# Weight loads in longer runs per partition, in a decode block that streams 185.6 MB

## The chip, the cores and the metric

The kernel runs on one core of one Trainium2 chip. The metric is device time in microseconds (us); lower is better. Every time below is a median over executions, and all of them were in the fast state. A kernel and the kernel before were run alternately on the same chip, and a ratio is the mean time of one kernel's fast runs over that of the other's in the same rounds, so it isn't quite the ratio of the medians that are quoted beside it.

## The reference, cut to what matters

One token passes through a conditioned layer norm, grouped-query attention over a long cache, and a gated feed-forward block. All tensors are bf16.

```python
mod = (silu(c) @ w_mod)                    # w_mod 1024 x 6144
h = layernorm(x) * (1 + ca) + sa
q = h @ wq                                 # wq 1024 x 4096: 32 heads of 128
p = softmax(q @ k.T * 128**-0.5)           # k, v: 4 kv heads x 65536 x 128
x = x + ga * ((p @ v) @ wo)                # wo 4096 x 1024
h = layernorm(x) * (1 + cb) + sb
x = x + gb * ((gelu(h @ w_gate) * (h @ w_up)) @ w_down)   # 1024 x 3584, 3584 x 1024
```

The K and V caches are 134.2 MB together; w_mod, wq, wo, gate, up and w_down are the other 51.4 MB. Each byte is read once.

## The kernel before

All large loads are issued by SP, in one order, into ten slots of 16 KB per partition. A load waits until the earlier users of its slots are done. Three small loads (c and x, 2 KB each) are issued by ACT on its own queue.

```python
def plan_load(src, view_fn, slot, site=None, nslot=1):   # nslot neighbouring slots
    ...
    for t in range(slot, slot + nslot):
        if last_job[t] is not None and last_job[t] not in job.prev:
            job.prev.append(last_job[t])
        last_job[t] = job

def issue_ready():                                       # strictly in the planned order
    while issued[0] < len(loads):
        j = loads[issued[0]]
        if any(q.freed is None for q in j.prev):
            return
        SP.wait(*(q.freed for q in j.prev))
        sp.dma_start(j.view, j.src).then_inc(j.tok[0], 16)
        issued[0] += 1
...
act.dma_start(c_in[:, :], c[0].rearrange("(p k) -> p k", p=P)).then_inc(c_sem, 16)      # 16 bytes per partition
act.dma_start(x_in[:, :], A_x[0, 0].rearrange("(p k) -> p k", p=P)).then_inc(x_sem, 16)
act.dma_start(x_row[:, :], A_x[0, 0].rearrange("(j p) -> j p", p=P)).then_inc(in_sem, 16)
wmod_v = w_mod.rearrange("(p k) n -> p k n", p=P)        # rows of one partition are neighbours in HBM
...                                                      # wq, wo, gate and up likewise
```

Since the rows of a partition lie together in HBM, a load of `k:k + n` is one contiguous run of n rows per partition. Before, w_mod takes 1 row (12 KB), wq 2 rows (16 KB), wo 8 (16 KB), gate and up 2 (14 KB). K is loaded in runs of 32 KB into two slots (0-1 and 2-3 in turn), V in runs of 16 KB into slots 4 to 7. TensorE's first instruction waits for x_row (until 10.49 us in the trace), and w_mod follows in the program (12.86 us).

## Time and profile before

| | before |
|---|---|
| time, median of 3 runs | 440.36 us |
| span of the profiled run | 438.8 us |
| load queue, share of 16 DMA engines | 98.8% |
| first weight packet starts / last one ends (packet records) | 1.85 / 435.67 us |

The page of the kernel before: its span, the busy time of each engine, the bytes moved in 40 equal slices, all DMA packets, and the load queue (packets, MB, and the share of the time of 16 engines that its packets took).

```profile
span 438.8 us, 15336 instructions
PE 351.7 (80%) x7107; PEld 318.4 (73%) x7107; DVE 176.2 (40%) x300; ACT 146.4 (33%) x553; POOL 11.7 (3%) x25
GB/s 332 427 435 428 430 429 432 432 433 425 430 445 420 453 414 455 408 445 438 410 448 415 445 419 442 427 435 432 430 437 424 439 423 433 432 427 431 424 425 237
DMA packets 11957, 185.89 MB, mean 424 GB/s; under 512 B 1568, under 2 KB 1568, under 8 KB 1952
q1 hardware_dynamic: 11632, 185.61, 98.8%
```

Apart from the first and the last slice, the rate is about the same in the slices of w_mod and wq (12 and 16 KB runs, the first five) as in those of K and V (single slices stray from 408 to 455, since a packet's bytes are counted whole in the slice where it starts). While loads are queued, differences between these run lengths are too small to be seen here. The table by stretches of this trace has 429 to 436 GB/s in stretches of 40 to 60 us from 20 to 400 us, and the page 424 GB/s over the whole span.

The timeline of TensorE in the kernel before, three parts of it (start, length, engine, line, operation, tiles, count, and in brackets the idle time just before it and what ended that):

```profile
10.49 0.16 PE L463 MATMUL b<-ident,x_row 8*128 8x8 bf16 x1 [10.49 <-DMA x_row<-in_A_x_dram]
12.86 4.78 PE L392 MATMUL kt_ps<-slots,s_pad 128*32 128x512 bf16 x36
...
63.04 1.88 PE L561 MATMUL kt_ps<-ident,slots 128*128 128x128 bf16 x16 [5.08 <-DMA slots<-in_A_k_cache_dram]
...
423.86 1.85 PE L372 MATMUL b<-u_col,slots 128*128 128x1 bf16 x64 [0.49 <-DVE u_col L841]
428.64 1.86 PE L372 MATMUL b<-u_col,slots 128*128 128x1 bf16 x64 [2.93 <-DMA slots<-in_B_w_down_dram]
433.51 2.91 PE L372 MATMUL b<-u_col,slots 128*128 128x1 bf16 x96 [3.01 <-DMA slots<-in_B_w_down_dram]
```

TensorE starts w_mod at 12.86 us, then waits for data. The first transpose of K (L561) waits 5 us for K to land, and the last third of w_down waits 3 us: at these two points data come last, so a lag of TensorE that is shorter than the wait is absorbed there.

The small loads of the kernel before, from the list of DMA issues (last number: us from issue to landing):

```profile
c_in<-in_c_dram ACTq DMA_DIRECT2D x1, 2.0 KB, 4.3
x_in<-in_A_x_dram ACTq DMA_DIRECT2D x1, 2.0 KB, 8.2
```

They are 2 KB each, and take as long as some 1.8 and 3.5 MB of the stream (an estimate, at the page's mean of 424 GB/s).

### The profile page before, as it was taken

How to read it: one execution, taken by the hardware profiler on the slowest of the kernel's cores; microseconds unless marked ns; L12 is line 12 of the kernel's file. 1: busy time of each engine (PE TensorE's matmuls, PEld its weight loads, DVE VectorE, ACT ScalarE, POOL GpSimd, SP SyncE). 2: the span in 40 equal slices, each digit the busy share in tenths (PEclk: the TensorE clock that was granted, in tenths of full speed). 3: DMA queues.
4: the chain of work that ended last, by engine and by line, in shares of the span. 5: the costliest groups of instructions: out<-in, count | busy, mean ns of one | idle time of the engine just before them, and what ended most of it. 6: DMA issues, size and time to landing. Idle time of an engine off the chain costs nothing.

```text
span 438.8 us, 15336 instructions
## 1 busy us (share of the span) xinstructions
PE 351.7 (80%) x7107; PEld 318.4 (73%) x7107; DVE 176.2 (40%) x300; ACT 146.4 (33%) x553; POOL 11.7 (3%) x25
## 2 busy tenths in 40 slices
PE   0547449998989889898799989999989999557554
PEld 0214139998989879798799989899988999434234
DVE  4102013545444644455444466345563365142100
ACT  1000001343435634344613553444654434600000
POOL 8100000000000000000000000000000000000000
PEclk9955555959777986869955899556995597659855
DMA  8999999999999999999999999999999999999995
GB/s 332 427 435 428 430 429 432 432 433 425 430 445 420 453 414 455 408 445 438 410 448 415 445 419 442 427 435 432 430 437 424 439 423 433 432 427 431 424 425 237
DMA packets 11957, 185.89 MB, mean 424 GB/s; under 512 B 1568, under 2 KB 1568, under 8 KB 1952
## 3 DMA queue, kind: packets, MB, share of 16 engines
q1 hardware_dynamic: 11632, 185.61, 98.8%
q8 instruction: 13, 0.21, 0.2%
q10 hardware_dynamic: 304, 0.01, 0.0%
q14 instruction: 8, 0.07, 0.0%
HBM read 185.60 MB, written 0.00 MB: 423 GB/s over the span
## 4 chain that ended last, share of the span: by engine, by line
DMA 60%; PE 35%; DVE 2%; issue 1%; SPq 1%; ACT 1%; POOL 0%
DMA slots<-in_A_v_cache_dram 39%; PE kt_ps L561 18%; DMA slots<-in_A_k_cache_dram 10%; DMA slots<-in_B_w_down_dram 7%; PE b L625 7%; PE sc_ps L581 6%; DMA slots<-in_w_mod_dram 4%; PE kt_ps L392 2%; PE b L605 1%; SPq L234 1%; PE b L372 1%; ACT p_sb L691 1%; PE b L595 1%; DVE kt_sb L751 0%; PE sc_ps L453 0%
## 5 line engine op out<-in xcount | busy, mean ns | idle before, releaser
L561 PE MATMUL kt_ps<-ident,slots 128*128 128x128 bf16 x2048 | 179.5, 258 | 11.0 <-DMA slots<-in_A_k_cache_dram 10.3
L561 PEld LDWEIGHTS kt_ps<-ident,slots 128*128 128x128 bf16 x2048 | 154.9, 118 | 12.7 <-issue 9.8
L660 DVE COPY kt_sb<-kt_ps 128x2048 bf16<-128x2048 bf16 x96 | 117.6, 1225 | 108.6 <-PE kt_ps L561 108.5
L660 ACT ACTIVATE kt_sb<-kt_ps 128x2048 bf16<-128x2048 bf16 x32 | 60.1, 1877 | 183.3 <-PE kt_ps L561 183.3
L625 PE MATMUL b<-p_sb,slots 128*128 128x8 bf16 x2176 | 75.8, 168 | 20.6 <-DMA slots<-in_A_v_cache_dram 11.2
L625 PEld LDWEIGHTS b<-p_sb,slots 128*128 128x128 bf16 x2176 | 69.8, 100 | 23.3 <-DMA slots<-in_A_v_cache_dram 12.3
L691 ACT ACTIVATE p_sb<-sc_ps,mneg 128x64 bf16<-128x64 f32 x256 | 83.5, 560 | 3.9 <-DVE mneg L686 3.9
L691 ACT ACTIVATION_READ_ACCUMULATOR p_sb<-sc_ps,mneg 128x1 f32 x256 | 77.1, 365 | 0.0
L581 PE MATMUL sc_ps<-q_buf,kt_sb 128*128 128x8 bf16 x2112 | 69.9, 167 | 0.5 <-issue 0.5
L581 PEld LDWEIGHTS sc_ps<-q_buf,kt_sb 128*128 128x128 bf16 x2112 | 67.9, 100 | 0.6 <-issue 0.6
L392 PE MATMUL kt_ps<-slots,h_pad 128*32 128x512 bf16 x176 | 17.1, 510 | 14.3 <-DMA slots<-in_A_wq_dram 6.3
L684 DVE TENSOR_REDUCE mg<-b 8x1 f32<-8x128 f32 x32 | 8.9, 279 | 37.1 <-PE b L595 37.1
L679 DVE TENSOR_REDUCE m_col<-sc_ps 128x8 f32<-128x512 f32 x32 | 21.8, 681 | 4.7 <-PE sc_ps L581 4.7
L392 PEld LDWEIGHTS kt_ps<-slots,h_pad 128*32 128x32 bf16 x176 | 5.0, 112 | 24.1 <-DMA slots<-in_A_wq_dram 8.3
L392 PE MATMUL kt_ps<-slots,s_pad 128*32 128x512 bf16 x96 | 12.5, 553 | 9.3 <-DMA slots<-in_w_mod_dram 9.3
L392 PEld LDWEIGHTS kt_ps<-slots,s_pad 128*32 128x32 bf16 x96 | 3.6, 119 | 17.3 <-DMA slots<-in_w_mod_dram 12.6
L605 PE MATMUL b<-negi,mg 8*128 8x8 f32 x66 | 15.8, 309 | 0.0
L605 PEld LDWEIGHTS b<-negi,mg 8*128 8x128 f32 x66 | 12.7, 239 | 2.2
L453 PEld LDWEIGHTS sc_ps<-identf,kt_sb 128*128 128x128 f32 (+1 forms) x48 | 7.6, 204 | 8.2 <-DVE kt_sb L774 4.3
L453 PE MATMUL sc_ps<-identf,kt_sb 128*128 128x128 f32 (+1 forms) x48 | 9.1, 352 | 4.5 <-DVE kt_sb L774 2.4
L686 DVE COPY mneg<-b 128x8 f32<-128x8 f32 x32 | 5.3, 167 | 18.1 <-PE b L605 18.1
L372 PE MATMUL b<-u_col,slots 128*128 128x1 bf16 x224 | 6.6, 165 | 6.5 <-DMA slots<-in_B_w_down_dram 5.9
(97 smaller groups left out, 84.9 us busy)
## 6 DMA issues: line engine op xcount, KB each, us to landing
slots<-in_A_k_cache_dram SPq DMA_DIRECT2D x16, 4096.0 KB, 20.3
slots<-in_A_v_cache_dram SPq DMA_DIRECT2D x32, 2048.0 KB, 26.5
slots<-in_w_mod_dram SPq DMA_DIRECT2D x8, 1536.0 KB, 17.5
slots<-in_A_wq_dram SPq DMA_DIRECT2D x4, 2048.0 KB, 35.2
slots<-in_A_wo_dram SPq DMA_DIRECT2D x4, 2048.0 KB, 32.5
slots<-in_B_w_gate_dram SPq DMA_DIRECT2D x4, 1792.0 KB, 21.9
slots<-in_B_w_up_dram SPq DMA_DIRECT2D x4, 1792.0 KB, 23.6
slots<-in_B_w_down_dram SPq DMA_DIRECT2D x3, 2048.0 KB, 29.1
```

What stands on the lines that cost most here:

```text
L372: ins = pe.matmul(bank[:, j:j + 1], view[:, kk, j * P:(j + 1) * P], rhs[:, k0 + kk:k0 + kk + 1], start=first, stop=True, skip_group_check= ...
L392: ins = pe.matmul(out, pad[:, k, :], jb.view[:, kk, c0:c0 + ROW], start=k <= last_k[0], stop=k >= last_k[1], skip_group_check=True,)
L453: ins = pe.transpose(dst[:, i * w:i * w + n], src[:, a], identf[0:src.shape[0], 0:n])
L561: ins = pe.transpose(kt_ps[:, half * 2048 + t * P:half * 2048 + (t + 1) * P], j_k[i - i % KU].view[:, i % KU * CH + b * TB + t, :], ident[ ...
L581: ins = pe.matmul(sc_ps[:, base + n * REP:base + (n + 1) * REP], kt_sb[:, j % 2, n, :], q_buf[:, j % SITES, :], start=True, stop=True,)
L605: ins = pe.matmul(b6[:, 256:256 + REP], mg8[:, j % 2:j % 2 + 1].to_broadcast([REP, P]), negi[:, :], start=True, stop=True,)
L625: ins = pe.matmul(b7[:, s * REP:(s + 1) * REP], j_v[j].view[:, n, :], p_sb[:, s, n, :], start=(n == 0), stop=(n == CH - 1),)
L660: ev[i % SITES][b].done(act.activation(dst, src, ACT.Copy) if E_ is AC else dve.tensor_copy(dst, src))
L679: m1[s].done(dve.tensor_reduce(m_col[:, j % 2, :].unsqueeze(2), scv, AX.X, ALU.max))
L684: m2[s].done(dve.tensor_reduce(mg8[:, j % 2:j % 2 + 1], b6[0:REP, 32:32 + P], AX.X, ALU.max))
L686: v_mc[j] = DVE.done(dve.tensor_copy(mneg[:, j, :], b6[:, 256:256 + REP]))
L691: ins = act.activation(p_sb[:, s, :, h], scv[:, h, :], ACT.Exp, bias=mneg[:, j, h:h + 1], scale=scale, accum_out=z_all[:, j, h:h + 1],)
```

## The change

Its intent is to give each packet more bytes, so that a fixed cost per packet (about 5 ns by the packet records and runs below) is paid less often: one load takes two or four rows of each partition and fills two slots. K, V and w_down keep their runs.

```diff
-        head = [8, 9, 0, 1, 2, 4, 3, 5, 6, 7, 8, 9]
-        j_mod = [(plan_load(wmod_v[:, k:k + 1, :], flat(1, M6), head[k]), k, 1) for k in range(KD)]
-        j_q = [(plan_load(wq_v[:, k:k + 2, :], flat(2, HQ * DH), head[KD + k // 2]), k, 2) for k in range(0, KD, 2)]
+        head = iter([8, 0, 2, 4, 6, 8])
+        j_mod = [(plan_load(wmod_v[:, k:k + 2, :], flat(2, M6), next(head), nslot=2), k, 2) for k in range(0, KD, 2)]
+        j_q = [(plan_load(wq_v[:, k:k + 4, :], flat(4, HQ * DH), next(head), nslot=2), k, 4) for k in range(0, KD, 4)]
 ...
-            return (plan_load(wo_v[:, k:k + 8, :], flat(8, D), next(tail)), k, 8)
+            return (plan_load(wo_v[:, k:k + 16, :], flat(16, D), next(tail), nslot=2), k, 16)
 ...
-        j_g = [(plan_load(wg_v[:, k:k + 2, :], flat(2, F), next(tail)), k, 2) for k in range(0, KD, 2)]
-        j_u = [(plan_load(wu_v[:, k:k + 2, :], flat(2, F), next(tail)), k, 2) for k in range(0, KD, 2)]
+        j_g = [(plan_load(wg_v[:, k:k + 4, :], flat(4, F), next(tail), nslot=2), k, 4) for k in range(0, KD, 4)]
+        j_u = [(plan_load(wu_v[:, k:k + 4, :], flat(4, F), next(tail), nslot=2), k, 4) for k in range(0, KD, 4)]
 ... (slot numbers of the tail and of w_down to suit)
```

More of the change, by code (lines that the diff above doesn't have):

```diff
@@ L111, in bass_adaLN_cond__gqa_block_cached__geglu_ffn__decode_kernel @@
     NQ = P // QD
-    assert FD % UE == 0 and M6 <= SLOT and KD % 2 == 0
+    assert FD % UE == 0 and M6 <= SLOT and KD % 4 == 0
     assert D == 2 * ROW and HQ * DH == 2 * NQ * ROW and F % ROW == 0 and F <= 2 * NQ * ROW and UE * P == ROW
@@ L263, in kv_src @@
             return h[g][:, cc * CH:(cc + n) * CH, :]
-        head = [8, 9, 0, 1, 2, 4, 3, 5, 6, 7, 8, 9]
-        j_mod = [(plan_load(wmod_v[:, k:k + 1, :], flat(1, M6), head[k]), k, 1) for k in range(KD)]
-        j_q = [(plan_load(wq_v[:, k:k + 2, :], flat(2, HQ * DH), head[KD + k // 2]), k, 2) for k in range(0, KD, 2)]
-        tail = iter([8, 9] + 2 * [0, 1, 2, 3, 4, 5, 6, 7, 8, 9])
+        head = iter([8, 0, 2, 4, 6, 8])
+        j_mod = [(plan_load(wmod_v[:, k:k + 2, :], flat(2, M6), next(head), nslot=2), k, 2) for k in range(0, KD, 2)]
+        j_q = [(plan_load(wq_v[:, k:k + 4, :], flat(4, HQ * DH), next(head), nslot=2), k, 4) for k in range(0, KD, 4)]
+        tail = iter([8, 0, 2, 4, 6, 8])
+        tail_d = iter([0, 1, 2, 3, 4, 5])
         def plan_o(k):
-            return (plan_load(wo_v[:, k:k + 8, :], flat(8, D), next(tail)), k, 8)
+            return (plan_load(wo_v[:, k:k + 16, :], flat(16, D), next(tail), nslot=2), k, 16)
         blank = {}
@@ L288, in emit_all @@
             if i == SITES:
-                j_o = [plan_o(k) for k in range(0, 16, 8)]
+                j_o = [plan_o(k) for k in range(0, 16, 16)]
             if i < NC and i % KU == 0:
@@ L294, in emit_all @@
                 j_v[j] = plan_load(kv_src(vh, j), flat(CH, DH), SITES + j % SITES, vfill[j % SITES])
-        j_o += [plan_o(k) for k in range(16, HQ, 8)]
-        j_g = [(plan_load(wg_v[:, k:k + 2, :], flat(2, F), next(tail)), k, 2) for k in range(0, KD, 2)]
-        j_u = [(plan_load(wu_v[:, k:k + 2, :], flat(2, F), next(tail)), k, 2) for k in range(0, KD, 2)]
+        j_o += [plan_o(k) for k in range(16, HQ, 16)]
+        j_g = [(plan_load(wg_v[:, k:k + 4, :], flat(4, F), next(tail), nslot=2), k, 4) for k in range(0, KD, 4)]
+        j_u = [(plan_load(wu_v[:, k:k + 4, :], flat(4, F), next(tail), nslot=2), k, 4) for k in range(0, KD, 4)]
         j_d = []
@@ L304, in emit_all @@
                 lambda t: t[:, 0:2 * UE * D].rearrange("p (b e n) -> p b e n", b=2, e=UE),
-                next(tail),
+                next(tail_d),
             )
@@ L310, in emit_all @@
             for e, ne in ((0, 2), (2, 1), (3, 1)):
-                jb = plan_load(wd_v[:, b, e:e + ne, :], flat(ne, D), next(tail))
+                jb = plan_load(wd_v[:, b, e:e + ne, :], flat(ne, D), next(tail_d))
                 j_d.append((jb, jb.view, b * UE + e, ne))
```

## The prediction

> **What bounds the kernel now.** DMA traffic. The page's queue table gives the load queue 98.8% of the time of 16 engines over 438.8 us (433.5 us); the table by stretches shows 420 to 438 GB/s in nearly every stretch from 5 to 430 us. [...] The first packet starts at 1.85 us, the last weight packet ends at 435.7 us, so about 5 us lie outside the stream. TensorE (80% busy) is close behind, but the chain of waits is mostly DMA (60%), and the queue stayed full behind its PE parts.
>
> **What longer runs save.** In the trace's packet records one packet is one run of one partition. Median times lie on a line: 8 KB 309 ns, 12 KB 460, 14 KB 535, 16 KB 611, 32 KB 1,213: 36.8 ns per 1,000 bytes plus about 9 ns per packet. So 12 KB already runs at 26.7 bytes/ns against 27.0 at 32 KB. [...] The K cache already uses 32 KB runs; K and V, 73% of the bytes, don't change. The change removes 512 (w_mod) + 256 (wq) + 256 (wo) + 512 (gate, up) = 1,536 packets, 96 per engine, 0.9 us at 9 ns (estimate from the fit), and 12 issues with their semaphore packets (12 per engine, 9 ns each: 0.1 us). Together about 1.0 us. SP's saved issue time (12 x about 0.4 us) is off the path.
>
> **What it costs.**
> - Head: the first w_mod load lands about 3.6 us later, but TensorE started w_mod only at 12.85 us, waiting for other inputs. The last w_mod and wq jobs process twice the rows after landing: +1.9 us at most for wq (16 matmuls took 1.90 us). q is ready near 60.3 us instead of 58.4; the first K transpose waited for K until 63.0. Absorbed.
> - Slots in pairs: issue times against bytes landed show about 2.8 to 4.4 MB still queued at each K and V refill, over 6 us of work. At the tail, the first up load moves from 380.4 to about 385.8 us with some 6 MB queued; the second waits for wo as before (396.2). w_down issues move by up to 4 us with 9 MB queued. No stall.
> - Tail: up's last job has 28 matmuls instead of 14, so w_down's column work starts about 1.7 us later; it had waited for data until 433.5. Absorbed.
>
> **On the critical path:** only the packet overhead, 1.0 us of 440.36.
>
> **Predicted: 439.4 us, 8 in 10 between 438.6 and 440.6.** Chances: faster by over 2% 0.01, within 2% 0.97, slower 0.02.
>
> **What would show it right:** packets down by about 1,700; load-queue busy time from 433.5 to about 432.5 us; 24 KB packets near 913 ns, 28 KB near 1,063; last w_down landing about 1 us earlier; first K transpose still waiting for K near 62 us.
>
> **What would make it wrong:** a stretch with DMA idle near 385 to 415 us, where two-slot loads wait for TensorE; runs cut into shorter packets (no gain); a lower granted clock, so that TensorE lags by more than the queued 6 us; engines that finish more unevenly (their last packets spread over 431.3 to 435.7 us now), so that the slowest gains less than the mean.

## The result, and the profile after

The changed kernel took 439.97 us (six runs, 439.87 to 440.27) against 440.44 us (six runs, 440.32 to 440.66): 0.47 us less, ratio 0.999, 95% interval 0.9978 to 1.0003. The interval of the ratio reaches from 0.97 us less to 0.1 us more: it excludes neither no gain nor, quite, the 1.0 us forecast. That the gain is half of the forecast can't be read from these two medians alone; the packet records suggest why it should be, and runs with a larger effect test it.

The same lines of the page after the change:

```profile
span 438.6 us, 15324 instructions
PE 345.6 (79%) x7107; PEld 315.0 (72%) x7107; DVE 171.9 (39%) x300; ACT 146.4 (33%) x553; POOL 11.7 (3%) x25
GB/s 343 411 442 429 428 432 426 430 432 427 429 435 429 448 420 456 410 445 439 410 451 409 452 409 451 418 433 442 424 434 427 433 430 433 438 434 425 423 424 238
DMA packets 10228, 185.88 MB, mean 424 GB/s; under 512 B 1376, under 2 KB 1376, under 8 KB 1760
q1 hardware_dynamic: 9904, 185.60, 98.8%
```

The load queue has 1,728 packets fewer, exactly 1,536 runs and 12 times 16 semaphore packets (a semaphore packet is a record of 4 bytes that follows a load's data, 16 to a load; in this trace the 16 semaphore updates of c's load come about 0.5 us after its 16 such records, at 10.26 to 10.73 us). The share of busy time didn't move in its last digit, and the last weight packet ends at 435.41 us instead of 435.67.

The timeline of TensorE after the change, at the same places:

```profile
20.18 0.16 PE L464 MATMUL b<-ident,x_row 8*128 8x8 bf16 x1 [20.18 <-DMA x_row<-in_A_x_dram]
20.78 7.09 PE L393 MATMUL kt_ps<-slots,s_pad 128*32 128x512 bf16 x72
...
63.24 1.89 PE L562 MATMUL kt_ps<-ident,slots 128*128 128x128 bf16 x16 [3.37 <-DMA slots<-in_A_k_cache_dram]
...
425.22 1.87 PE L373 MATMUL b<-u_col,slots 128*128 128x1 bf16 x64 [0.44 <-DVE u_col L842]
428.36 1.87 PE L373 MATMUL b<-u_col,slots 128*128 128x1 bf16 x64 [1.27 <-DMA slots<-in_B_w_down_dram]
433.36 2.82 PE L373 MATMUL b<-u_col,slots 128*128 128x1 bf16 x96 [3.13 <-DMA slots<-in_B_w_down_dram]
```

Two things are to be seen. First, w_mod starts 8 us later, because x_row lands at 20 us instead of 10, which nothing in the diff names (the first w_mod rows had landed at 10.5 us and silu(c) was ready at 11.95, but w_mod stands behind x_row in TensorE's program). Second, it costs nothing: the first K transpose still waits 3.4 us for K, and starts within 0.2 us of where it did. At the end w_down's first matmuls are 1.4 us later, and the last third waits for data as before.

The small loads after the change:

```profile
c_in<-in_c_dram ACTq DMA_DIRECT2D x1, 2.0 KB, 10.0
x_in<-in_A_x_dram ACTq DMA_DIRECT2D x1, 2.0 KB, 17.2
```

A cause for half the gain shows in the packet records, once not the durations but the times from one packet's start to the next one's on the same engine are read (most frequent values, successive packets of the same size, ns; 24 KB and 28 KB from the changed kernel, the others from the kernel before; the kept records name no engine, so a packet counts as the next one where it starts within some ns of another's end):

```
bytes     recorded duration   start to next start
 2,048           84                  80
 4,096          159                 155
 8,192          309                 306
14,336          535                 532
16,384          611                 607   (613 where a semaphore packet lies between)
24,576          912                 908 to 914
28,672        1,062               1,059
32,768        1,213               1,209
```

Records of successive packets overlap by 3 to 4 ns. From the starts, 16,384 further bytes cost 602 ns, so a packet costs 607 - 602 = 5 ns beyond its bytes, not the 9 ns that a line through the durations gives, and a semaphore packet costs 6. The slope, 16,384 bytes in 602 ns, is 27.2 bytes/ns per engine, or 435 GB/s over 16 engines, near the 429 to 436 GB/s of the stretches. Then 96 packets and 12 semaphore packets per engine are 0.57 us (with 5.2 and 5.7 ns, the figures that the expectations below use), close to the 0.47 us measured. A line through the start-to-start times of all sizes from 2 to 32 KB gives 4.7 ns per packet and 5.9 per semaphore packet, so 0.52 us. This is theory C of the experiments. Rivals are theory A (9 ns per packet is right, and half of the gain is given back in the first 20 us, where long packets meet the empty stream and the small loads) and theory B (the loss is at the tail, through loads in pairs of slots).

Theory A had some support. In the two profiles, the time of packets beyond the fit through the durations, summed and divided by 16 engines, was 0.46 us in the first 20 us before, and 0.96 us after.

### The profile page after: what moved, and what is told of

It reads as the page before. It is cut to its first block, busy times and chain, and to the rows that moved or that the text cites. A ratio compares the mean times of both kernels' runs of the same rounds, so it can differ in the third digit from the quotient of the medians.

```text
span 438.6 us, 15324 instructions
## 1 busy us (share of the span) xinstructions
PE 345.6 (79%) x7107; PEld 315.0 (72%) x7107; DVE 171.9 (39%) x300; ACT 146.4 (33%) x553; POOL 11.7 (3%) x25
## 4 chain that ended last, share of the span: by engine, by line
DMA 57%; PE 37%; DVE 2%; issue 2%; ACT 1%; SPq 1%; ACTq 0%; POOL 0%
DMA slots<-in_A_v_cache_dram 39%; PE kt_ps L562 18%; DMA slots<-in_A_k_cache_dram 8%; PE b L626 7%; DMA slots<-in_B_w_down_dram 6%; PE sc_ps L582 6%; DMA x_row<-in_A_x_dram 4%; PE kt_ps L393 3%; PE b L606 1%; PE b L373 1%; ACT p_sb L692 1%; PE b L596 1%; SPq L234 1%; DVE kt_sb L752 0%; PE sc_ps L454 0%
## 5 line engine op out<-in xcount | busy, mean ns | idle before, releaser
L562 PE MATMUL kt_ps<-ident,slots 128*128 128x128 bf16 x2048 | 176.7, 256 | 10.2 <-DMA slots<-in_A_k_cache_dram 9.5
L562 PEld LDWEIGHTS kt_ps<-ident,slots 128*128 128x128 bf16 x2048 | 152.6, 117 | 12.0 <-issue 6.6
L626 PEld LDWEIGHTS b<-p_sb,slots 128*128 128x128 bf16 x2176 | 68.8, 99 | 26.2 <-issue 12.8
L393 PEld LDWEIGHTS kt_ps<-slots,h_pad 128*32 128x32 bf16 x176 | 6.1, 124 | 24.8 <-issue 11.2
L464 PE MATMUL b<-ident,x_row 8*128 8x8 bf16 x1 | 0.2, 161 | 20.2 <-DMA x_row<-in_A_x_dram 20.2
L606 PE MATMUL b<-negi,mg 8*128 8x8 f32 x66 | 14.9, 296 | 0.0
L393 PE MATMUL kt_ps<-slots,s_pad 128*32 128x512 bf16 x96 | 10.7, 516 | 4.9 <-DMA slots<-in_w_mod_dram 4.9
```

Source lines behind the costliest of these rows:

```text
L393: ins = pe.matmul(out, pad[:, k, :], jb.view[:, kk, c0:c0 + ROW], start=k <= last_k[0], stop=k >= last_k[1], skip_group_check=True,)
L562: ins = pe.transpose(kt_ps[:, half * 2048 + t * P:half * 2048 + (t + 1) * P], j_k[i - i % KU].view[:, i % KU * CH + b * TB + t, :], ident[ ...
L606: ins = pe.matmul(b6[:, 256:256 + REP], mg8[:, j % 2:j % 2 + 1].to_broadcast([REP, P]), negi[:, :], start=True, stop=True,)
L626: ins = pe.matmul(b7[:, s * REP:(s + 1) * REP], j_v[j].view[:, n, :], p_sb[:, s, n, :], start=(n == 0), stop=(n == CH - 1),)
```

## The experiments

### One part of the change alone, and two changes to the head

**Head only**: w_mod and wq in long runs; all the rest as before.

```diff
 the kernel before, with the `head`, `j_mod` and `j_q` lines of the change
```

> Long runs for w_mod and wq only; wo, gate, up as before. Theory A (each packet costs about 9 ns on its engine, and about half of the gain is given back in the first 20 us, where the first packets and the small loads of c and x meet longer packets): 768 packets fewer, 48 per engine, is -0.5 us, given back by +0.5 us: 440.4, no change against before. Rival B (the packets' gain is kept at the head, and the loss sits at the tail, where loads in pairs of slots make TensorE late): 439.9. Both: c lands near 10 us and x_row near 20 us, as in the changed kernel.

Measured: 440.30 us against 440.50 (ratio 0.9995, interval 0.9982 to 1.0009). c landed 6.1 us after its issue, earlier than expected, and x_row at 16.3 us. The packet time beyond the fit in the first 20 us was 0.52 us, not 0.96, although the head is the same code as in the changed kernel. So that surplus varies from execution to execution. Over all kept profiles it doesn't follow the length of the first packets either: recounted with the usual duration of each size, it is 0.45 to 0.95 us (mean 0.62) in the seven kernels whose first packets have 12 KB, and 0.54 to 0.97 (mean 0.72) in the seven with longer ones. The 0.5 us that theory A needs stands between the first two profiles, but not between the two groups.

**Tail only**: wo, gate and up in long runs; w_mod and wq as before.

```diff
 the changed kernel, with the `head`, `j_mod` and `j_q` lines of before
```

> Long runs for wo, gate and up only; w_mod and wq as before. Theory A: 768 packets and 6 issues fewer, nothing given back: -0.5 us, 439.9. Rival B: the tail gives its gain back: 440.4. Both: x_row lands near 10 us, as in the kernel before.

Measured: 440.61 us against 440.50 (ratio 1.0002, interval 0.9989 to 1.0016). Theory C expects -0.28 us from each half (48 packets and 6 semaphore packets), and -0.20 and +0.11 were measured. With intervals of 0.6 us either way these two runs can't tell C from A or B. By its median the tail's half favours B, and it is answered only by the single-row run below, which enlarges the same effect on wq, wo, gate and up.

**Short start**: the changed kernel, with rows 0 and 1 of w_mod as two loads of 12 KB runs.

```diff
-        head = iter([8, 0, 2, 4, 6, 8])
-        j_mod = [(plan_load(wmod_v[:, k:k + 2, :], flat(2, M6), next(head), nslot=2), k, 2) for k in range(0, KD, 2)]
+        head = iter([0, 2, 4, 6, 8])
+        j_mod = [(plan_load(wmod_v[:, k:k + 1, :], flat(1, M6), 8 + k), k, 1) for k in range(2)]
+        j_mod += [(plan_load(wmod_v[:, k:k + 2, :], flat(2, M6), next(head), nslot=2), k, 2) for k in range(2, KD, 2)]
```

> The changed kernel, but rows 0 and 1 of w_mod as two loads of 12 KB runs, so that the first packets are short again. Theory A: the extra packet time of the first 5 us falls from about 0.7 to 0.4 us per engine, at 8 packets more per engine (0.08 us): 0.2 us less than the changed kernel, 439.8. Rival B: no less than the changed kernel, 440.0. The small loads still meet 24 KB packets: x_row lands after 15 us.

Measured: 439.97 us (439.54 to 440.27), the same as the changed kernel's 439.97; no gain from the short start is shown. The expectation that x_row lands after 15 us was wrong: TensorE's wait for it ended at 10.27 us, as in the kernel before. The two short loads are 16 packets per engine, as many as the turns that c and x can need (next section).

**Small loads in line**: the changed kernel, with the loads of c and x issued by SP after the first w_mod load, on the same queue.

```diff
             issued[0] += 1
+            if issued[0] == 1:
+                sp.dma_start(c_in[:, :], ...)      # and x_in, x_row
-        act.dma_start(c_in[:, :], ...)             # and x_in, x_row
```

> The changed kernel, but the three small loads of c and x are issued on SP's queue after the first w_mod load, not on ACT's queue beside it, so that their 16-byte packets don't take turns with 24 KB packets. Theory A: TensorE's wait for x_row falls from 20.2 us to about 9 or 10, its first w_mod matmul comes near 11 us instead of 20.8; the extra packet time at 10 to 20 us (0.23 us per engine) goes; total 439.8. If the late x cost nothing at all in the stream, 440.0 as the changed kernel. Rival B: 440.0.

Measured: 440.30 us against 440.50 (ratio 0.9993, interval 0.9979 to 1.0007). TensorE's wait for x_row ended at 11.20 us and w_mod started at 12.86, close to what was expected. Nothing was gained, since the data come last at 63 us in either case. The late x was real in the changed kernel, and not on the path.

### Why x is late, and how late it may be

In the packet records of the changed kernel the packets of c and x, 16 bytes each, start 16 at a time, one group every 0.91 to 1.01 us, where a 24 KB packet takes 0.91: as if each engine took turns between the two queues, a single record at a time. c and x have 8 packets of 16 bytes each per engine (128 records each, over 16 engines). If each has to wait for one packet of the weight stream, x needs 16 turns: 16 x 0.46 = 7.3 us with 12 KB runs, 16 x 0.91 = 14.6 with 24 KB runs, and 29 with 48 KB runs (estimates from the recorded 460 and 912 ns, the last with twice 912). x_in took 8.2 and 17.2 us from its issue. A run with 48 KB runs tests it.

**w_mod in 48 KB runs**:

```diff
-        head = iter([8, 0, 2, 4, 6, 8])
+        head = iter([0, 3, 6, 8])
-        j_mod = [... wmod_v[:, k:k + 2, :], flat(2, M6), next(head), nslot=2 ...
+        j_mod = [... wmod_v[:, k:k + 4, :], flat(4, M6), next(head), nslot=3 ...
```

> The changed kernel, but w_mod in two loads of 48 KB runs. Each 16-byte packet of c and x takes its turn after one long packet: c lands near 17 us, x_row near 34 (10 and 20 in the changed kernel, 5 and 10.5 before). TensorE starts w_mod near 35 us, q is ready near 64 to 66 instead of 60, just past the K landing at 63; the first K refill moves by 1 to 3 us with some 9 us of data queued. Time: as the changed kernel within 0.3 us, 440.0. If the late x is not absorbed: 442 or more.

Measured: 439.86 us (439.82 to 439.91) against 440.52 (ratio 0.9985, interval 0.9971 to 1.0). The small loads and TensorE in this run:

```profile
c_in<-in_c_dram ACTq DMA_DIRECT2D x1, 2.0 KB, 17.6
x_in<-in_A_x_dram ACTq DMA_DIRECT2D x1, 2.0 KB, 31.8
```

```profile
35.51 8.85 PE L393 MATMUL kt_ps<-slots,s_pad 128*32 128x512 bf16 x96
62.91 1.89 PE L562 MATMUL kt_ps<-ident,slots 128*128 128x128 bf16 x16 [4.47 <-DMA slots<-in_A_k_cache_dram]
```

x landed about where 16 turns put it (31.8 us from its issue, against 29). The packet records show the turns: the 256 packets of c and x start in 16 groups of 16, one group about every 1.82 us here and every 0.91 us in the changed kernel, one run apart. How many turns x needs isn't fixed: in head only and in the changed kernel with V in pairs, which begin as the changed kernel does, the first packets of c got in ahead of the weights, and x_in took 13.2 and 13.5 us instead of 17.2. w_mod started 23 us later than in the kernel before, and was worked through without a pause, as all of it had landed; q was ready at 58.9 us, earlier than I had expected, and the first K transpose still waited 4.5 us for K. So even this delay is absorbed.

**w_mod in one 96 KB load**, to delay x until it must cost something, and **the same with c and x first**:

```diff
-        head = iter([8, 0, 2, 4, 6, 8])
+        head = iter([0, 6, 8])
-        j_mod = [... wmod_v[:, k:k + 2, :], flat(2, M6), next(head), nslot=2 ...
+        j_mod = [... wmod_v[:, k:k + 8, :], flat(8, M6), next(head), nslot=6 ...
 and in the second kernel c_in, x_in and x_row are issued with sp.dma_start instead of act.dma_start
```

> The changed kernel, but w_mod in one load of 96 KB runs. Theory D (each 16-byte packet of c, x and x_row waits for one packet of the weight stream on its engine, so a longer run delays all of TensorE's start): c lands near 31 us (8 turns of 3.6 us), x_row near 43 (9 further turns with 32 KB packets of wq); TensorE starts w_mod near 44 us; the first K load, which needs w_mod's slots, is issued near 55, after the 21 MB queued at the start have drained near 51; the stream stands idle for 5 us or more: 446 to 450. If only the size of the load matters and not the turns, x lands near 20 us as in the changed kernel, and the time stays near 440. The packets saved are 24 per engine, 0.15 us.

> The same with c, x and x_row issued on SP's queue ahead of w_mod. Theory D: they land by 5 us, TensorE starts w_mod when it lands near 33 us, K is issued near 44 with data still queued, no idle stretch; the stream starts about 1.3 us later for the three issues: 441. If the 96 KB load itself is the trouble (one landing for all of w_mod): 444 or more.

Measured: 439.97 us (439.83 to 441.57; ratio 1.0002, interval 0.9986 to 1.0018) and 440.99 us (440.84 to 441.35; ratio 1.0016, interval 1.0000 to 1.0031) against 440.36. The first expectation failed: the load was cut into packets of 49,152 bytes (1,815 ns each) and c slipped in ahead of the weights (landed 1.9 us after its issue), so x needed fewer turns and landed at 22 us. This run didn't reach the point at which a late x costs time, and that point stays open. The second kernel came out as expected: x was early, TensorE waited for w_mod until 34 us, and the weight stream, issued about 1.3 us later, ended later too (last packet at 436.48 us instead of 435.39 in the first). Here the early x, bought with a later stream, was a loss of about 1 us between the medians, at the edge of what the intervals can tell.

### What a packet costs on the path

These runs enlarge the suspected cost. **K in eighths** and **K in halves** cut each K load of the kernel before into 8 or 2 loads of shorter runs, with the same slots and waits:

```diff
-            sp.dma_start(j.view, j.src).then_inc(j.tok[0], 16)
+            m = j.view.shape[1] // j.parts
+            for a in range(j.parts):
+                sp.dma_start(j.view[:, a * m:(a + 1) * m, :] if j.parts > 1 else j.view,
+                             j.src[:, a * m:(a + 1) * m, :] if j.parts > 1 else j.src).then_inc(j.tok[0], 16)
 ... (the semaphore targets of K are multiplied by 8 or 2)
```

> The kernel before, but each K load is cut into eight loads of 4 KB runs: 14,336 packets and 112 loads more, 896 packets and 112 semaphore packets per engine. Theory A (the intercept of the packet durations, 9 ns, is what a packet costs): +9.2 us, 449.7. Theory C (packets of one engine overlap by about 4 ns; from start to start a 16 KB packet takes 607 ns and a 32 KB packet 1,209, so a packet costs 5.2 ns and a semaphore packet about 5.7): +5.3 us, 445.8. Theory of no effect (the stream is bound by bytes alone): 440.5.

> The kernel before, with each K load cut into two loads of 16 KB runs: 128 packets and 16 semaphore packets more per engine. Theory C (5.2 ns per packet, 5.7 per semaphore packet): +0.76 us, 441.25. Theory A (9 ns each): +1.3 us, 441.8. Bytes alone: 440.5.

**Single rows** reverses the change and goes further: wq, wo, gate and up one row of each partition at a time.

```diff
-            nfill[slot] += 1
+            nfill[slot] += parts
-            sp.dma_start(j.view, j.src).then_inc(j.tok[0], 16)
+            for a in range(j.parts):
+                sp.dma_start(j.view[:, a:a + 1, :] if j.parts > 1 else j.view,
+                             j.src[:, a:a + 1, :] if j.parts > 1 else j.src).then_inc(j.tok[0], 16)
 ... (parts=2 for wq, gate and up, parts=8 for wo)
```

> The kernel before with the change reversed: wq, wo, gate and up are loaded one row of each partition at a time (8, 2, 7 and 7 KB runs) into the same slots, w_mod stays at 12 KB: 5,120 packets and 40 loads more, 320 packets and 40 semaphore packets per engine. Theory C (5.2 and 5.7 ns each, from start to start): +1.9 us, 442.3. Theory A (9 ns, from the durations): +3.3 us, 443.7. If weight packets at the head and the tail are not on the path and only K and V are (which the tail alone, without a gain, could hint at): 440.4.

Measured (C and A are what the two theories expected; the cost is the measured difference over all packets added per engine, semaphore packets included):

| | this, us | before, us | difference | C | A | cost per packet added |
|---|---|---|---|---|---|---|
| K in eighths, +1,008 per engine | 445.33 | 440.52 | +4.81 | +5.3 | +9.2 | 4.8 ns |
| K in halves, +144 | 441.31 | 440.36 | +0.95 | +0.76 | +1.3 | 6.6 ns |
| single rows, +360 | 442.29 | 440.54 | +1.75 | +1.9 | +3.3 | 4.9 ns |
| the change, -108 | 439.97 | 440.44 | -0.47 | -0.57 | -1.0 | 4.4 ns |

The load queue of K in eighths, from its page:

```profile
q1 hardware_dynamic: 27760, 185.61, 99.6%
```

With K loads of 0.5 MiB, queued behind each other, this run moved 419 GB/s on average; the kernel before, with K loads of 4 MiB, moved 424.

Theory C holds over a range of nine in the number of packets. Theory A falls: with more than twice the packets of the kernel before, 4.8 ns each were paid (the intervals of the ratios are 4.2 to 5.6 us for K in eighths and 1.2 to 2.4 us for single rows, so A's 9.2 and 3.3 lie outside). K in halves can't tell the two apart (interval 0.3 to 1.5 us). The single-row run shows that the packets of wq, wo, gate and up, taken together (3,584 of the 5,120 are wo's), cost as those of K do, so weights at the head and the tail are on the path like everything else in the stream. That answers the part of theory B by which the tail's packets don't count. A loss of some tenths of a microsecond by pairs of slots at the tail isn't excluded by the time of the tail-only run. The packet records exclude it for the executions that were profiled: from 20 to 430 us none of the 16 DMA engines was without a packet for more than 0.01 us on average, in the kernel before, the changed kernel, tail only and the three other runs of this table alike. So the cut loads didn't leave the queue empty either, and their extra time is packet time. The share on the page hides a trap: the sum of recorded durations rose by 8.5 us here (442.2 us per engine instead of 433.7), while the time rose by 4.8, because the records overlap.

### Would longer runs elsewhere pay more?

V is 36% of the bytes and has 4,096 runs of 16 KB. **V in pairs** loads two V pieces at once into two slots, in runs of 32 KB, alone and with the change.

```diff
-                j_v[j] = plan_load(kv_src(vh, j), flat(CH, DH), SITES + j % SITES, vfill[j % SITES])
+                j_v[j] = plan_load(kv_src(vh, j, 2), flat(2 * CH, DH), SITES + j % SITES, vfill[j % SITES // 2], 2)   # even j only
-                    pwait(vfill[s], j, it)
+                    if j % 2 == 0:
+                        pwait(vfill[s // 2], j, it)
 ... (both pieces are released after the second)
```

> The kernel before, but V is loaded in pairs, 32 KB runs into two slots: 2,048 packets and 16 loads fewer, 128 packets and 16 semaphore packets per engine. Theory A: -1.3 us, 439.2. Theory C: -0.76 us, 439.7. If two-slot loads cost something in the loop: no gain or a loss. Each V refill was already issued next to the following one, so no stall is expected.

> The changed kernel and V in pairs: 3,584 packets and 28 loads fewer than before. Theory A: -2.3 us, 438.2. Theory C: 0.57 + 0.76 = 1.3 us less, 439.1 (439.3 if the first 20 us give back what they did in the changed kernel).

Measured: V in pairs alone 441.37 us (439.59 to 444.25), ratio 1.0021, interval 0.9996 to 1.0046; with the change 439.98 us (439.51 to 441.85), ratio 0.9989, interval 0.9976 to 1.0002; before 440.52. Neither kept the expected gain, and their executions scatter over some 2 to 5 us, where the kernel before has 0.5. The table by stretches (last numbers: granted clock, DMA share, GB/s), from 280 to 320 us, of the kernel before and then of the profiled run of V in pairs, which was its slowest at 444.25 us:

```profile
280.00:320.00 40.00, 38.67 (x807) 37.90 (x804) 20.34 (x34) 17.43 (x68) 0.00 (x0) 0.70 1.01 432
```

```profile
280.00:320.00 40.00, 35.66 (x761) 34.96 (x759) 18.63 (x30) 17.54 (x68) 0.00 (x0) 0.74 0.99 418
```

TensorE's waits for V, first before and then with V in pairs (us in total, times, longest):

```profile
PE b L625 <- DMA slots<-in_A_v_cache_dram: 11.2, 12, 2.0
```

```profile
PE b L618 <- DMA slots<-in_A_v_cache_dram: 25.5, 11, 5.1
```

The rate fell from 432 to 418 GB/s although the packets were longer, and TensorE waited 14 us more for V. Bytes issued less bytes moved, taken at each K refill from the issue times and the packet records, suggest why: 3.8 MB were queued in the median and 2.7 MB at least before, but 1.9 MB in the median and 0.5 MB at least with V in pairs. A pair is usable only when both halves have landed, and its slots come free only when both have been used, so the queue runs thin. The packet records agree: between 20 and 430 us each engine was without a packet for 1.07 us in this execution (0.00 before), and packets took 3.15 us longer than their usual durations (0.56 before), most of it near 245, 304, 344 and 363 us, at four of the five refills that found some 1.4 MB or less queued (packets under way counted as queued). That is one execution, the slowest; the fastest ones, 439.59 and 439.51 us, come near theory C, and no experiment changed the depth of the queue alone. My expectation that V in pairs would cause no stall looked only at the issue times of neighbouring refills. In the changed kernel itself the queue didn't thin: 4.0 MB in the median, 2.9 MB at least.

No kernel tried here beats the changed one by more than the scatter; with 48 KB runs for w_mod (439.86 us) the time is the same.

## Why the prediction was right or wrong, point by point

- **The bound and the time.** Right that the stream of bytes sets the time, that only the packet overhead is on the path, and that the change would be far within 2%. 439.97 us lies within the stated range, above the stated 439.4.
- **"Plus about 9 ns per packet", and so 1.0 us.** This is the term that was mis-sized. Packet records overlap by 3 to 4 ns; from start to start a packet costs about 5 ns, and by the time of the enlarged runs 4.8 and 4.9. That makes 0.52 to 0.57 us for the change, and 0.47 was measured. The mechanism (fewer packets, the bytes unchanged, all else absorbed) was right; this one term was twice too large. "Load-queue busy time to about 432.5 us" failed too: it went from 433.7 to 433.3, the fitted part falling by 0.99 us and the surplus in the first 20 us rising by 0.5 in that execution. That surplus ranges as widely in kernels whose first packets are short (head only, above), and no run ties it to the time.
- **Packets and their durations.** 1,728 fewer, as said; 24 KB took 912 ns (913 said), 28 KB 1,062 (1,063 said). No run was cut, up to 48 KB.
- **Head.** "TensorE started w_mod only at 12.85 us, waiting for other inputs" was true before, but the argument took those inputs as fixed. The change moved them: x_row landed at 20.2 us instead of 10.5, and w_mod started at 20.8. The verdict "absorbed" held all the same: q was ready at 60.3 us as said, and K was waited for until 63.2 (62 was said).
- **Tail and slots.** The first up load was issued at 386.2 us (385.8 said), the second at 396.7 (396.2 said), w_down's matmuls started 1.4 us later (1.7 said), and the stream moved 429 GB/s from 360 to 430 us (428 before), with no engine idle. No stall, as said. The last w_down landing gained less than 1 us: the last matmul group starts 0.15 us earlier, and the last weight packet ends 0.26 us earlier, in one execution of each.

## What to carry to other kernels

Where a deep queue of loads kept the DMA engines busy, as here, a longer run saved about 5 ns per packet and nothing else, so count packets per engine before the change is written; of a 12 KB packet (457 ns from start to start) that is about 1%, and this is the most that longer runs could save (an estimate from these figures). Take the cost per packet from start to start, or from a run with many more packets, and not from recorded durations, which overlap. Ask also what a longer packet or a coarser load does to others: small loads on another queue waited for one long packet at each turn here (x_in took 8.2, 17.2 and 31.8 us beside runs of 12, 24 and 48 KB), and buffers that came free in pairs cost more in some executions than the packets saved.
